# Conformer block on one core: the first chunk's blocks per tile, the last tile in two halves, and one gate multiply moved from GpSimd to VectorE

## The chip, the cores and the metric

The kernel runs on one core of one Trainium2 chip. The metric is the device time of one execution in microseconds (us), as the median of several executions. Each run also leaves a profile of one execution, with the clock that TensorE was granted.

## The reference, cut to what matters

The kernel computes one Conformer block in bf16 on x of shape (2, 4000, 512), with a feed-forward width of 2048 and a depthwise convolution of three taps.

```python
h = _layernorm(x);   x1 = x + 0.5 * (_silu(h @ w_ff1_a) @ w_ff1_b)
h = _layernorm(x1)
attn = softmax((h @ w_q) @ (h @ w_k).T * scale) @ (h @ w_v) @ w_o
x2 = x1 + attn
a, b = split(_layernorm(x2) @ w_pw1)
h = a * _sigmoid(b)                                  # the "gate"
dc = sum(pad(h)[:, i:i + T, :] * dw[i] for i in range(3))   # depthwise, taps dw
dc = (dc - mu) / sqrt(var + 1e-05)                   # mu, var over ALL 8000 rows
x3 = x2 + _silu(dc) @ w_pw2
x4 = x3 + 0.5 * (_silu(_layernorm(x3) @ w_ff2_a) @ w_ff2_b)
return _layernorm(x4)
```

(Abridged; `...` and the batch dimension are left out.) The mean and variance over all rows are what makes a join: nothing behind the convolution can start before the convolution's last chunk has its statistics.

## The kernel before

The 8000 rows are 16 chunks of 500, each of four tiles of 125 rows; the 512 features are four blocks of 128. TensorE is fed from a hand-made order, so the order in the program is the order on each engine.

The start: the first chunk is normalised tile by tile, transposed through TensorE, and its first four blocks of the first product are made as tiles come in.

```python
def head(self):
    self.warm(14)
    self.early = [self.sbank() for _ in range(4)]
    def blocks(lo, hi):                       # tiles lo..hi-1 of the first four blocks
        for f, (ps, b_ps) in enumerate(self.early):
            out = ps[:, lo * TILE:hi * TILE].rearrange("p (t k) -> p t k", t=hi - lo)
            for cc in range(DC):
                self.mm(out, self.Wa[:, cc, f * 128:(f + 1) * 128], self.lnT[0][:, lo:hi, cc, 0:TILE], ...)
    for ti in self.ln_tiles(0, 0, lag=1):
        if ti:
            self.transpose_pe(ti - 1, 0, "ACT", ...)
        if ti == 2:
            blocks(0, 1)
    blocks(1, 2)
    self.transpose_pe(TPC - 1, 0, "DVE", ...)
    blocks(2, 4)
```

The join. `conv_b` and `conv_a` are the two halves of `w_pw1` for one block of features, `gate` is a times sigmoid(b), and `depthwise` is three matmuls with diagonal weights and returns a VectorE statistic and a ScalarE copy. `tail` is the last chunk but one.

```python
def prepare(ti):
    self.project(last, ti)
    if ti == 0:
        self.conv_b(tail, DC - 2)
    if ti == 2:
        self.conv_a(tail, DC - 2)              # gate of block 2, on GpSimd
for ti in self.ln_tiles(last, ..., prepare, ("ACT", "ACT", "DVE", "DVE")):
    if ti == TPC - 3:
        self.conv_b(tail, DC - 1)
        gate = self.conv_a(tail, DC - 1)       # gate of block 3, on VectorE, later
drains = [self.depthwise(tail - 1, self.KEEP)]
for k in range(2):
    self.transpose_pair(k, 1, ("ACT", "DVE")[k], ybank())
drains.append(self.depthwise(tail - 1, DC - 2))
gate()
...
def finish(cc):
    for t in (last, tail):
        f, copy = self.depthwise(t, cc)
        f(); copies.append(copy)
    self.conv_scale(cc)                        # aggregate on VectorE, power on GpSimd
for jj in range(DC):
    self.conv_b(last, jj)
    ...
    self.conv_a(last, jj)
    if jj > 1:
        self.conv_shift(jj - 2)                # needs that power
    if jj:
        finish(jj - 1)
    else: ...                                  # depthwise(tail - 1, DC - 1)
```

The end, `ff_last`: for each tile 16 matmuls of 512 columns, then residual, statistics, factor and normalisation, then the store.

```python
for ti in range(TPC):
    for f in range(FC):
        self.ff_second(f, ti, *blocks[f], f == FC - 1)
    self.residual(...); self.ln_stats(...); self.ln_mean(...); self.ln_factor(...)
    self.ln_norm(c, sl, ti, self.osb[0][:, ti, :], self.b_osb[0][ti], "DVE")
    self.store_out(c, self.osb[0], self.b_osb[0], ti, ti + 1, ("SP", "ACT"))
```

## Time and profile before

| | before |
|---|---|
| time, median of 3 (lowest to highest) | 2060.52 us (2060.18 to 2060.56) |
| span of the profiled execution | 2056.5 us |
| TensorE (PE) busy | 2044.2 us, 99% |
| granted clock over the span | 0.999 |
| VectorE / ScalarE / GpSimd busy | 54% / 36% / 6% |

With TensorE at 99%, the busy shares say nothing on what a small reordering is worth. The list of TensorE's waits does, and the timelines around each wait say who ends it. The prediction shows these lines.

### The profile page before, as it was taken

What the parts mean: (1) busy time and instruction counts of PE and PEld (TensorE: products, weight loads), DVE (VectorE), ACT (ScalarE), POOL (GpSimd) and SP (SyncE); (2) the same over time, 40 slices, a digit from 0 to 9 for tenths busy, and PEclk for the clock granted to TensorE, in tenths of its full rate; (3) what the DMA queues carried; (4) which work ended last, traced back from release to release, by engine and by line L of the source; (5) the groups of instructions that cost most, each with busy time, mean ns of one, the idle gap of its engine ahead of it and who ended that gap; (6) DMA issues with size and microseconds to landing.
All of it is one profiled execution on the core that took longest, in us unless ns stands there. A gap on an engine that the chain in (4) does not pass through costs nothing.

```text
span 2056.5 us, 24392 instructions
## 1 busy us (share of the span) xinstructions
PE 2044.2 (99%) x9653; PEld 1037.7 (50%) x9653; DVE 1110.0 (54%) x2274; ACT 744.3 (36%) x1270; POOL 128.7 (6%) x275
## 2 busy tenths in 40 slices
PE   9999999999999999999999999999999999999998
PEld 5555555554444444444444444444445555555554
DVE  4244444325556667666666676667764443443443
ACT  3433333333333333333333333333345443443432
POOL 2012100000000000000000000000011000000000
PEclk9999999999999999999999999999999999999999
DMA  7232221110001100114301010101143111111111
GB/s 181 54 62 57 56 61 49 46 49 11 16 6 24 24 16 18 21 23 110 92 17 24 18 24 14 23 18 24 38 129 93 31 31 41 31 31 41 31 31 42
DMA packets 209324, 87.73 MB, mean 43 GB/s; under 512 B 157873, under 2 KB 208692, under 8 KB 209204
## 3 DMA queue, kind: packets, MB, share of 16 engines
q1 hardware_dynamic: 208808, 85.79, 17.4%
q8 instruction: 78, 1.28, 0.3%
q14 instruction: 42, 0.34, 0.1%
q10 hardware_dynamic: 396, 0.31, 0.0%
HBM read 29.53 MB, written 19.04 MB: 24 GB/s over the span
## 4 chain that ended last, share of the span: by engine, by line
PE 98%; DVE 1%; issue 0%; POOL 0%; DMA 0%; SPq 0%; ACT 0%; POOLq 0%; DVEq 0%; ACTq 0%
PE s L465 55%; PE y L465 42%; DVE wff L1062 0%; DVE work L547 0%; DMA wff<-in_w_ff_a_dram 0%; DVE xt L680 0%; SPq L519 0%; DVE work L569 0%; POOL work L674 0%; POOL work L1071 0%; DVE wff L967 0%; DVE work L504 0%; ACT work L507 0%; PE y L493 0%; DVE work L1069 0%
## 5 line engine op out<-in xcount | busy, mean ns | idle before, releaser
L507 ACT ACTIVATE work<-s 128x500 bf16<-128x500 f32 (+1 forms) x1060 | 621.6, 587 | 1219.8 <-PE s L465 1218.2
L465 PE MATMUL s<-work,wff 128*128 128x500 bf16 (+2 forms) x2592 | 628.3, 373 | 2.5 <-DVE work L504 1.7
L465 PE MATMUL s<-work,keys 128*128 128x500 bf16 x2048 | 517.5, 374 | 0.1
L465 PE MATMUL y<-work,keys 128*128 128x500 bf16 x2048 | 514.4, 373 | 0.1
L465 PE MATMUL y<-wff,work 128*125 128x512 bf16 x2016 | 506.6, 379 | 0.0
L834 DVE TENSOR_TENSOR work<-work 128x500 f32<-128x500 f32 x496 | 334.4, 674 | 282.1 <-ACT work L507 279.2
L465 PEld LDWEIGHTS s<-work,wff 128*128 128x128 bf16 x2592 | 251.9, 98 | 280.3 <-issue 2.1
L465 PEld LDWEIGHTS y<-wff,work 128*125 128x125 bf16 x2016 | 275.2, 137 | 173.5
L465 PEld LDWEIGHTS y<-work,keys 128*128 128x128 bf16 x2048 | 199.2, 97 | 234.4 <-DVE work L899 1.1
L465 PEld LDWEIGHTS s<-work,keys 128*128 128x128 bf16 x2048 | 199.8, 98 | 232.2 <-DVE work L763 0.6
L680 DVE SCALAR_TENSOR_TENSOR xt<-y,xt 125x512 bf16<-125x512 f32 x128 | 79.7, 683 | 343.8 <-PE y L465 343.8
L547 DVE BATCH_NORM_STATS2 work<-xt 125x6 f32<-125x512 bf16 x316 | 199.7, 680 | 7.9 <-DMA xt<-in_x_dram 7.7
L556 POOL TENSOR_TENSOR work<-work 125x4 f32<-125x4 f32 x76 | 77.0, 1013 | 1115.2 <-DVE work L554 1115.2
L465 PE MATMUL s<-work 128*125 128x512 bf16 (+3 forms) x524 | 133.5, 379 | 2.1 <-DVE work L1172 1.3
L569 DVE TENSOR_SCALAR work<-xt,work 125x512 bf16<-125x512 bf16 x279 | 111.7, 444 | 16.8 <-POOL work L556 13.0
L680 DVE SCALAR_TENSOR_TENSOR xt<-s,xt 125x512 bf16<-125x512 f32 x56 | 38.7, 692 | 146.4 <-PE s L465 146.4
L465 PEld LDWEIGHTS s<-work 128*125 128x125 bf16 (+2 forms) x524 | 70.3, 136 | 47.9 <-issue 3.5
L680 DVE SCALAR_TENSOR_TENSOR xt<-s,work,xt 125x512 bf16<-125x512 f32 x64 | 48.0, 751 | 32.6 <-PE s L465 32.0
L465 PE MATMUL s<-keys,work 128*128 128x500 bf16 x256 | 64.4, 376 | 0.0
L971 DVE SCALAR_TENSOR_TENSOR wff<-wff,s 128x500 bf16<-128x500 f32 x57 | 38.6, 678 | 43.5 <-PE s L465 41.5
L507 ACT ACTIVATE wff<-s 128x500 f32<-128x500 f32 x67 | 39.2, 586 | 57.2 <-PE s L465 55.2
L507 ACT ACTIVATE work<-keys,work 128x500 bf16<-128x500 bf16 x64 | 50.4, 794 | 1.1 <-DVE work L1076 1.1
(89 smaller groups left out, 493.8 us busy)
## 6 DMA issues: line engine op xcount, KB each, us to landing
xt<-in_x_dram SPq DMA_DIRECT2D x15, 500.0 KB
out_dram<-work SPq DMA_DIRECT2D x15, 500.0 KB
dcvd<-wff SPq DMA_DIRECT2D x52, 125.0 KB, 1.7
keys<-dcvd SPq DMA_DIRECT2D x13, 500.0 KB, 4.4
wff<-in_w_ff_a_dram SPq DMA_DIRECT2D x16, 256.0 KB, 4.4
keys<-work SPq DMA_DIRECT2D x8, 512.0 KB, 3.6
keys<-keys SPq DMA_DIRECT2D x32, 128.0 KB, 2.1
work<-work SPq DMA_TRANSPOSE x210, 2.5
```

Source lines behind the costliest of these rows:

```text
L465: self.S.op("PE", lambda e: e.matmul(out, lhsT, rhs, start=start, stop=stop), reads=reads, writes=[bank], inc=stop if inc is None else inc)
L507: return self.S.op("ACT", lambda e: e.activation(out, in_, func, **kw), reads=reads, writes=writes)
L547: self.S.op("DVE", lambda e: e.bn_stats(self.st[sl][:, ti, :], x), reads=[b_x], writes=[self.b_st[sl][ti]])
L556: S.op("POOL", lambda e: e.tensor_tensor(out=self.rs[sl], in0=self.va[sl], in1=self.neghalf[0:TILE, :], op=ALU.pow), reads=self.b_va[sl] + ...
L569: self.S.op("DVE", lambda e: e.tensor_scalar(out, x, self.mv[sl][:, ti, 0:1], self.rs[sl][:, ti:ti + 1], ALU.subtract, ALU.mult), reads=[b ...
L680: self.S.op("DVE", lambda e: e.scalar_tensor_tensor(out=self.XT[g], in0=ps, scalar=scalar, in1=self.XT[g], op0=ALU.mult, op1=ALU.add), rea ...
L834: S.op("DVE", lambda e, p=p: e.tensor_tensor(out=self.acc[s], in0=self.acc[s], in1=self.P[p], op=ALU.add), reads=[self.b_P[p], self.b_acc[ ...
L971: self.S.op("DVE", lambda e: e.scalar_tensor_tensor(out=out, in0=self.th[k], scalar=1.0, in1=ps[:, 0:CHUNK], op0=ALU.add, op1=ALU.mult), r ...
```

## The change

Its intent is to shorten three places in which TensorE waits. At the start each tile's 16 small matmuls run as soon as that tile is there. At the join one gate multiply moves from GpSimd to VectorE, three depthwise matmuls leave the wait in front of the last chunk and each shift moves behind the next statistic. At the end the last tile's second product is made in two halves of 256 columns, so that half of the residual and of the statistics runs beside the other half's matmuls.

```diff
-        def blocks(lo, hi):
+        def blocks(ti):
...
-                    self.mm(out, ..., self.lnT[0][:, lo:hi, cc, 0:TILE], ...
+                    self.mm(ps[:, ti * TILE:(ti + 1) * TILE], ..., self.lnT[0][:, ti, cc, 0:TILE], ...
...
-            if ti == 2:
-                blocks(0, 1)
-        blocks(1, 2)
+            if ti > 1:
+                blocks(ti - 2)
         self.transpose_pe(TPC - 1, 0, "DVE", (self.Yb[TPC - 1], self.b_Y[TPC - 1]))
-        blocks(2, 4)
+        blocks(TPC - 2)
+        blocks(TPC - 1)
... (ff_last: the last tile)
+        for n in range(2):
+            d = slice(n * D // 2, (n + 1) * D // 2)
+            ps, b_ps = self.Yb[(0, ti)[n]], self.b_Y[(0, ti)[n]]
+            ... 16 matmuls into ps[0:TILE, d], residual and bn_stats of those columns
+            if n == 0:
+                out(TPC - 2)
+        ... one aggregate over both statistics, factor, out(ti)
... (join)
-            if jj < DC - 1:
+            if jj < DC - 2:
                 return gate("POOL")
             return lambda: gate("DVE")
...
-            if ti == 2:
-                self.conv_a(tail, DC - 2)
+            if ti == 1:
+                gates.append(self.conv_a(tail, DC - 2))
...
-        drains.append(self.depthwise(tail - 1, DC - 2))
-        gate()
+        for gate in gates:
+            gate()
...  (in finish)
+                if t == last and cc > 1:
+                    self.conv_shift(cc - 1)
...
-                f, copy = self.depthwise(tail - 1, DC - 1)
-                f()
-                copies.append(copy)
+                for cc in (DC - 2, DC - 1):
+                    f, copy = self.depthwise(tail - 1, cc)
+                    f()
+                    copies.append(copy)
```

## The prediction

> **What bounds the kernel now.** I read the engines' busy time first, then TensorE's waits, then the timelines around those waits. Columns of the timelines: start, us, engine, line, operation, output<-inputs, count, [idle before <- releaser].

> ```profile
> PE 2044.2 (99%) x9653; PEld 1037.7 (50%) x9653; DVE 1110.0 (54%) x2274; ACT 744.3 (36%) x1270; POOL 128.7 (6%) x275
> ```

> ```profile
> PE s L465 <- DVE work L504: 1.7, 3, 0.9
> PE s L465 <- DVE work L1172: 1.3, 1, 1.3
> PE s L465 <- ACT work L507: 1.0, 2, 0.8
> PE y L493 <- ACT work L507: 1.0, 1, 1.0
> PE s L465 <- DMA wff<-in_w_ff_a_dram: 0.6, 1, 0.6
> ```

> TensorE is busy 2044.2 of 2056.5 us, and the span's granted clock is 0.999. The waits listed (total, times, longest) and two of 0.4 and 0.3 us sum to 6.3 us; with 5.3 us after TensorE's last matmul (2051.17 to 2056.5), where only VectorE, GpSimd and a store still run, that is all that any reordering can win: under 0.6%. All these waits lie in three places: the first 13 us, the join between attention and the second feed-forward (1535 to 1564 us), and the last 6 us. The change touches exactly these. Everything between runs TensorE back to back, so what is won in one place should reach the end.

> Start, the blocks of the first chunk:

> ```profile
> 10.74 0.39 PE L480 MATMUL y<-work 125*128 125x125 bf16 x4
> 11.16 0.42 DVE L504 COPY work<-y 128x500 bf16<-128x500 bf16 x1 [2.21 <-PE y L480]
> 11.73 2.73 PE L465 MATMUL s<-work,wff 128*128 128x250 bf16 x20 [0.61 <-DVE work L504]
> 12.36 2.73 ACT L507 ACTIVATE work<-s 128x500 bf16<-128x500 f32 x5 [1.71 <-PE s L465]
> ```

> The blocks of tiles 2 and 3 (16 matmuls of 250 columns) wait together for the copy of tile 3, though tile 2 was ready at 10.64.

> The join:

> ```profile
> 1533.06 1.25 POOL L957 TENSOR_TENSOR wff<-wff 128x500 bf16<-128x500 f32 x1 [0.21 <-ACT wff L507]
> 1533.57 0.75 DVE L620 SCALAR_TENSOR_TENSOR work<-work 125x1 f32<-125x1 f32 x1
> ...
> 1551.54 0.25 DVE L1069 BATCH_NORM_AGGREGATE work<-wff 128x2 f32<-128x21 f32 x1
> ...
> 1551.87 0.55 POOL L1071 TENSOR_TENSOR work<-work 128x1 f32<-128x1 f32 x1 [1.49 <-DVE work L1069]
> ...
> 1552.52 0.16 DVE L1076 SCALAR_TENSOR_TENSOR work<-work 128x1 f32<-128x1 f32 x1 [0.73 <-POOL work L1071]
> ...
> 1556.06 1.08 PE L465 MATMUL s<-work 128*125 128x512 bf16 x4 [0.84 <-ACT work L507]
> ```

> Two stalls of VectorE: an instruction on one column takes 0.75 us and ends (1534.32) just after GpSimd's gate multiply (1534.31); and VectorE idles 0.73 us between the aggregate of block 2 and its shift, because the shift needs a GpSimd power. The chain of waits runs along VectorE from there to the swish that releases TensorE at 1556.06.

> End: the last tile's residual, statistics and so on are serial after TensorE's last matmul.

> ```profile
> 2049.24 1.89 PE L465 MATMUL y<-wff,work 128*125 128x512 bf16 x8
> ...
> 2051.17 0.69 DVE L680 SCALAR_TENSOR_TENSOR xt<-y,xt 125x512 bf16<-125x512 f32 x1 [0.55 <-PE y L465]
> 2051.89 0.69 DVE L547 BATCH_NORM_STATS2 work<-xt 125x6 f32<-125x512 bf16 x1
> 2052.62 0.18 DVE L667 BATCH_NORM_AGGREGATE work<-work 125x2 f32<-125x6 f32 x1
> ```

> [...] The trace's start-to-start times agree: 54.5, 107.3, and 215.5 for 512. [...] weight loads of 125 columns show 137 ns against 98 for 128. Even so both overlap the matmuls, so halving the columns should not bring the load on the path: eight matmuls of one column with 125-column weights stand 58.3 ns apart, under 109. [...] The 746 ns above against 148 to 160 for its six siblings agrees. [...] The trace agrees in slope: 683 ns for 512 columns, 150 for one.

> **The start.** With tile 2 alone, its 16 matmuls follow the transposes of tile 3 at about 10.96 and take 16 x 0.0545 = 0.87, to 11.83. Tile 3's copy ends at 11.58 and releases TensorE some 0.15 later (as before: 11.58 to 11.73), so the 16 of tile 3 run from 11.83 to 12.70 without waiting. Before, block 4 began at 11.73 + 16 x 0.1073 = 13.44. But block 4 needs the PSUM bank of block 0, which ScalarE frees: its first block is complete at 11.83 + 3 x 0.0545 + 0.22 = 12.21, the activation (0.59, 0.04 after) ends at 12.84, TensorE goes on at 12.98. Gain 0.74 - 0.28 = **0.46 us**. The next weights landed at 10.77 and later chunks land over 2 us before use, so no transfer takes it back.

> **The join.** (a) The gate of block 2 leaves GpSimd: 1245 ns less there, 671 on VectorE (as the gate of block 3 took), but placed behind the pair copy, where VectorE would soon wait. (b) conv_a of block 2 goes ahead of the projection of tile 2, which ends 0.86 later (1532.37 against 1531.51); VectorE reaches its residual at 1532.41 instead of 1532.13: a loss of 0.28. (c) The one-column instruction shrinks from 0.75 to 0.15: a win of 0.60. Sum to the last normalise and so to the pair copy: 0.32 earlier; the first matmuls of the last chunk start at 1538.36 instead of 1538.68. (d) Before, three depthwise matmuls (0.63 us) filled the wait in front of that copy. Now they follow the chunk's first eight matmuls, so the second eight start at 1538.36 + 1.70 + 1.27 = 1541.34 against 1541.03, and with them VectorE's second gate, which waits for exactly this: 1543.30 against 1542.99. The 0.32 are gone, and 0.31 lost. ScalarE gets to the first sigmoid one copy earlier, but that isn't the last wait here. (e) From there the chain gate, two statistics, aggregate, GpSimd power, halo, gate repeats as before, 0.31 late, to the last gate (1549.75 against 1549.44). (f) The shifts move behind the next statistics. Shift 1 waited for nothing and, between two statistics, hides a gap: the aggregate of block 2 starts 1551.77 against 1551.54. Shift 2's wait of 0.73 is now filled with a statistic of 0.68: statistic 1551.95 to 1552.63, shift at 1552.76, next statistic 1552.83 instead of 1553.31. So 0.48 won at the end of the chain, and the aggregate, power, shift and swish behind it keep that: swish at 1554.73 instead of 1555.21. ScalarE, with its copies and swishes, is free at 1554.3 by the same count, TensorE before that. The four swishes and normalisations that follow are back to back on ScalarE, hence shift along. Net **0.48 us**.

> **The end.** 32 matmuls x 0.1095 = 3.50 instead of 16 x 0.216 = 3.46: lose 0.05. The first half is complete about 1.75 us before the second; its residual and statistics (0.42 each) and the normalise of tile 2 (0.41) fit in, done at about 2050.8, before the second half at 2051.2. After the last matmul the residual and the statistics fall by 256 columns each[...]: win 0.53. The aggregate over two groups costs some 0.03 more (15 values took 0.222 us, 6 took 0.176). Net **0.45 us**.

> Sum: 0.46 + 0.48 + 0.45 = 1.39 us of 2060.52, so 2059.1.

> **Rivals.** (1) The join gives nothing or costs: (d) is a real loss on TensorE, and if the statistic that fills the wait of shift 2 has to wait for its own matmuls (they need ScalarE copies that stand behind an activation table load of 1.28 us), the win shrinks. For: before, TensorE waited at 1550.65 for just such a copy. Against: I place that copy's end at 1550.90 and the matmuls' at 1551.76, before the aggregate's end at 1552.02, but the slack is only 0.2 us. Time then 2059.6. (2) ScalarE keeps the start as it was: if the activation rather than the matmuls paced blocks 4 and on. Against: it starts one every 0.47 us there, TensorE asks every 1.7. For: half of the gain is already lost to it in my sum. Time 2059.3 to 2059.5. (3) The end gains more, if the store of tile 2, now nearer to the last one, doesn't matter, and less if weight loads show at 256 columns (32 x 28 ns, the gap between 137 and 109, would be 0.9 us, eating the whole half): 2060.0. The pitch of 58 ns speaks against it. (4) The join gains up to 0.9, if the second gate isn't as late as in (d), since ScalarE alone would allow the swish at 1554.3: 2058.7.

> **Range and chances.** Run to run is 0.4 us. Each part may be off by 0.2 to 0.4, mostly independently, so 0.7 each way: 2058.4 to 2059.9. All the waits together are under 0.6% and the added matmuls 16, so leaving the 2% band is all but excluded: 0.003 each way.

> **What would show it.** Right: no wait of TensorE on the VectorE copy near 11.8 but about 0.3 on ScalarE before block 4; no one-column instruction of 0.7 us; all gates from the second on about 0.3 later relative to the start of the join, and the swish of the last block 0.5 earlier; the last residual and statistics near 0.42 each. Wrong: a wait for weights at the start, TensorE's matmuls of 256 columns over 0.115 apart, or the last depthwise statistic waiting for TensorE.

54.5, 107.3 and 215.5 ns are the start-to-start times of matmuls of 125, 250 and 512 columns. The 109 ns for 256 columns (0.1095 us in the sum of the end) are my estimate, near the line from 107.3 to 215.5; the changed kernel's trace then had 109.2. That the instruction of 746 ns would shrink to 0.15 us is my estimate too, from its six siblings of 148 to 160 ns and from its end beside that of GpSimd's multiply; why it takes longer there was not shown. The 0.53 us of the end follow from 683 ns for 512 columns and 150 for one: 1.04 ns a column, so 0.267 us for 256 columns, twice.

## More of the kernel before

The taps of the convolution are loaded in the second chunk, and TensorE turns them round six steps later; the change doesn't touch this, the argument does:

```python
if c == 1 and f == 1:
    self.load(self.dwr, i["dw"], [self.b_dwr])
    self.after(6, self.taps)
```

Last, the whole program is followed by a conditional second program for data out of range, which doesn't run here. Each engine therefore ends by loading a flag and taking a branch:

```python
self.program(False)
fits = nc.values_load(self.flag, ...)
self.wait_out()
with nc.If(fits < 1):
    self.program(True)
```

## The result, and the profile after

The changed kernel took 2060.77 us (median of 4 runs: 2061.31, 2060.21, 2060.23, 2063.35), the kernel before 2060.54 us (2060.18 to 2060.61, 4 runs). A ratio in this document is the mean time of one kernel's runs over that of the other's of the same rounds, so it isn't quite the ratio of the medians: here 1.0004, with a 95% interval of 0.9987 to 1.0021. The predicted 2059.1 us and the range of 2058.4 to 2059.9 were wrong. None of the four runs lies in the range. Two of them, 1.1 and 3.1 us above the other two, differ by more than the kernel before's runs here.

First the page of the changed kernel, engines' busy time:

```profile
PE 2045.9 (99%) x9685; PEld 1039.7 (51%) x9685; DVE 1112.8 (54%) x2277; ACT 744.4 (36%) x1270; POOL 127.0 (6%) x274
```

The 32 more matmuls and the GpSimd instruction less are the change. But TensorE is busy for 1.7 us longer (2044.2 before), although 16 matmuls of 512 columns became 32 of 256. TensorE's waits in the changed kernel (total, times, longest):

```profile
PE s L465 <- DVE work L504: 1.7, 2, 0.9
PE s L465 <- DVE work L1196: 1.3, 1, 1.3
PE y L480 <- ACT work L507: 0.7, 1, 0.7
PE s L465 <- DMA wff<-in_w_ff_a_dram: 0.6, 1, 0.6
PE y L493 <- ACT work L507: 0.6, 1, 0.6
```

The wait on the tile copy near 11.8 us is gone (the first line had three waits, now two), and with it the wait of 0.8 us on a ScalarE swish at 1556 us. The total of the first line stays at 1.7 us because its other wait, in front of the last chunk of the join, grew from 0.23 to 0.87 us: step (d) of the prediction leaves it unfilled. So the waits went as foreseen and the time didn't. The timeline of the start, changed kernel (start, us, engine, line, operation, output<-inputs, count, [idle before <- releaser]):

```profile
11.15 3.04 PE L465 MATMUL s<-work,wff 128*128 128x125 bf16 x36
11.35 0.42 DVE L504 COPY work<-y 128x500 bf16<-128x500 bf16 x1 [2.23 <-PE y L480]
...
14.03 0.59 PE L465 MATMUL y<-wff,work 128*125 128x512 bf16 x2
```

The 16 matmuls of tile 2 run beside tile 3's copy, and those of tile 3 follow without a gap. From tile 3's transposes (10.93) to the first matmul of the second product (14.03) it is 3.10 us; before it was 3.56 (10.74 to 14.29, in rounded times).

At the join, the timeline of the changed kernel:

```profile
1533.58 0.15 DVE L620 SCALAR_TENSOR_TENSOR work<-work 125x1 f32<-125x1 f32 x1
...
1538.08 3.29 PE L465 MATMUL s<-work,wff 128*128 128x500 bf16 x8 [0.87 <-DVE work L504]
```

The one-column instruction takes 0.15 us instead of 0.75, and the first eight matmuls of the last chunk start earlier. But these eight take 3.29 us. The same eight before:

```profile
1538.68 1.86 PE L465 MATMUL s<-work,wff 128*128 128x500 bf16 x8 [0.23 <-DVE work L504]
```

The windows from 1538 to 1542 us say why. Columns: us, then PE, PEld, DVE, ACT and POOL busy with the count of instructions, the granted TensorE clock, DMA share, GB/s. Kernel before:

```profile
1538.00:1542.00 4.00, 3.77 (x19) 1.51 (x17) 2.87 (x5) 2.17 (x4) 0.45 (x4) 1.00 0.37 120
```

Changed kernel:

```profile
1538.00:1542.00 4.00, 3.92 (x11) 1.52 (x12) 2.23 (x4) 1.06 (x2) 1.07 (x6) 0.57 0.29 92
```

TensorE was as busy and did 11 matmuls instead of 19, because its clock was 0.57 of full speed on average. In the records of the clock it was 0.5 from 1538.33 us for 3.41 us, then full again.

The end, changed kernel:

```profile
2052.22 0.42 DVE L757 SCALAR_TENSOR_TENSOR xt<-y,xt 125x256 bf16<-125x256 f32 x1 [0.61 <-PE y L465]
2052.68 0.43 DVE L760 BATCH_NORM_STATS2 work<-xt 125x6 f32<-125x256 bf16 x1
2053.14 0.21 DVE L763 BATCH_NORM_AGGREGATE work<-work 125x2 f32<-125x12 f32 x1
```

Residual and statistics fell from 0.69 to 0.42 and 0.43 us as predicted. Yet the span ends 2.88 us after the last normalisation, which ends at 2054.62; before it was 2.42 us. The transfers in the two microseconds from that point (queue, kind, packets, MB, share of the 16 engines), kernel before and then changed kernel:

```profile
q1 hardware_dynamic: 96, 0.08, 17.0%
q10 hardware_dynamic: 60, 0.05, 6.9%
q14 instruction: 2, 0.02, 2.3%
```

```profile
q1 hardware_dynamic: 93, 0.08, 17.4%
q10 hardware_dynamic: 59, 0.05, 7.3%
q8 instruction: 1, 0.02, 3.8%
```

q1 and q10 carry the last store. Beside it the changed kernel has one packet of q8, an instruction fetch, that the kernel before does not have there, and of its 156 store packets only 152 fall in the window.

To see where time goes, I cut each trace at four marks: the first one-column matmuls of the last softmax sums, at the end of attention ("start", near 1525 us; called "the sums" below), the first of the second feed-forward ("join", near 1564), the end of the last normalisation ("last tile") and the end of the span ("store"). Each entry is the length of that stretch less its length in the kernel before, to about 0.01 us; the runs other than "after" are the experiments below.

| trace | start | join | last tile | store | sum |
|---|---|---|---|---|---|
| predicted | -0.46 | -0.48 | -0.45 | 0 | -1.39 |
| after | -0.27 | +1.22 | -0.40 | +0.47 | +1.02 |
| again | +0.74 | -0.47 | -0.39 | +0.21 | +0.09 |
| filled | +0.20 | -0.46 | -0.40 | +0.92 | +0.26 |
| head_tail | +0.34 | 0.00 | -0.40 | +0.81 | +0.75 |
| drain_moved | -0.59 | +0.60 | +0.01 | +0.08 | +0.10 |
| taps_later | -0.53 | -0.46 | -0.39 | +0.59 | -0.79 |
| tail_128_384 | -0.76 | -0.47 | -0.10 | +0.02 | -1.31 |
| tail_pad | -1.00 | -0.48 | -0.39 | -0.16 | -2.03 |
| fixed_pad | -0.97 | -0.45 | -0.40 | +0.08 | -1.74 |
| before_taps | -0.13 | +0.01 | +0.01 | +0.02 | -0.09 |
| join_alone | +0.21 | -0.46 | 0.00 | +0.08 | -0.17 |
| wait_1 | -0.88 | +0.27 | -0.39 | +0.50 | -0.50 |
| wait_1_again | -0.98 | +0.24 | -0.39 | +0.26 | -0.87 |
| wait_2 | -0.53 | +2.65 | -0.39 | +0.75 | +2.48 |
| wait_3 | -0.40 | +4.63 | -0.39 | +0.78 | +4.62 |
| wait_3_filled | -0.31 | +1.70 | -0.39 | +0.43 | +1.43 |

The start has a scatter of its own, since the first loads land at different times (TensorE waits 0.6 us for the first weights in the kernel before, 0.2 in before_taps, and drain_moved lists no such wait): drain_moved and before_taps have the old start and lie 0.5 us apart. So the start is better read from inside: tile 3's transposes to the first block of the second product took 3.56 us in all four traces with the old start and 3.10 in all thirteen with the new one. The predicted 0.46 us is there every time. From that block to the mark near 1525 us it is 1510.63 or 1510.64 us in fifteen of the seventeen traces, and 1511.96 and 1511.79 in again and head_tail, so the gain reaches the end of attention except in these two.

### The profile page after: what moved, and what is told of

It is laid out like the page before. It is cut to its first block, busy times and chain, and to the rows that moved or that the text cites. A ratio compares the mean times of both kernels' runs of the same rounds, so it can differ in the third digit from the quotient of the medians.

```text
span 2057.5 us, 24459 instructions
## 1 busy us (share of the span) xinstructions
PE 2045.9 (99%) x9685; PEld 1039.7 (51%) x9685; DVE 1112.8 (54%) x2277; ACT 744.4 (36%) x1270; POOL 127.0 (6%) x274
## 3 DMA queue, kind: packets, MB, share of 16 engines
q8 instruction: 78, 1.28, 0.3%
## 4 chain that ended last, share of the span: by engine, by line
PE 98%; DVE 1%; issue 0%; POOL 0%; DMA 0%; SPq 0%; ACT 0%; POOLq 0%; DVEq 0%; ACTq 0%
PE s L465 55%; PE y L465 42%; DMA wff<-in_w_ff_a_dram 0%; DVE work L547 0%; DVE wff L1086 0%; SPq L519 0%; DVE work L569 0%; POOL work L674 0%; POOL work L1095 0%; DVE xt L680 0%; DVE wff L991 0%; ACT work L507 0%; DVE work L504 0%; PE y L493 0%; DVE work L1093 0%
## 5 line engine op out<-in xcount | busy, mean ns | idle before, releaser
L507 ACT ACTIVATE work<-s 128x500 bf16<-128x500 f32 (+1 forms) x1060 | 621.8, 587 | 1219.1 <-PE s L465 1217.6
L465 PE MATMUL s<-work,wff 128*128 128x500 bf16 (+1 forms) x2608 | 629.9, 373 | 2.7 <-DVE work L504 1.7
L465 PE MATMUL s<-work,keys 128*128 128x500 bf16 x2048 | 517.5, 374 | 0.1
L465 PE MATMUL y<-work,keys 128*128 128x500 bf16 x2048 | 514.4, 373 | 0.1
L465 PE MATMUL y<-wff,work 128*125 128x512 bf16 (+1 forms) x2024 | 506.8, 378 | 0.0
L465 PEld LDWEIGHTS s<-work,wff 128*128 128x128 bf16 x2608 | 252.4, 98 | 280.8 <-issue 2.9
L465 PEld LDWEIGHTS y<-wff,work 128*125 128x125 bf16 x2024 | 275.9, 136 | 172.8
L465 PEld LDWEIGHTS y<-work,keys 128*128 128x128 bf16 x2048 | 199.2, 97 | 234.4 <-DVE work L923 1.1
L465 PEld LDWEIGHTS s<-work,keys 128*128 128x128 bf16 x2048 | 199.8, 98 | 232.2 <-DVE work L787 0.6
L680 DVE SCALAR_TENSOR_TENSOR xt<-y,xt 125x512 bf16<-125x512 f32 x127 | 79.1, 683 | 340.4 <-PE y L465 340.4
L547 DVE BATCH_NORM_STATS2 work<-xt 125x6 f32<-125x512 bf16 x315 | 199.1, 680 | 8.1 <-DMA xt<-in_x_dram 7.9
L465 PE MATMUL s<-work 128*125 128x512 bf16 (+3 forms) x524 | 133.3, 379 | 1.3 <-DVE work L1196 1.3
L680 DVE SCALAR_TENSOR_TENSOR xt<-s,xt 125x512 bf16<-125x512 f32 x56 | 38.7, 692 | 146.3 <-PE s L465 146.3
L465 PEld LDWEIGHTS s<-work 128*125 128x125 bf16 (+2 forms) x524 | 70.2, 136 | 47.0 <-issue 3.3
L680 DVE SCALAR_TENSOR_TENSOR xt<-s,work,xt 125x512 bf16<-125x512 f32 x64 | 48.1, 751 | 32.6 <-PE s L465 32.0
L465 PE MATMUL s<-keys,work 128*128 128x500 bf16 x256 | 64.4, 376 | 0.0
L507 ACT ACTIVATE wff<-s 128x500 f32<-128x500 f32 x67 | 39.2, 587 | 58.3 <-PE s L465 56.2
L507 ACT ACTIVATE work<-keys,work 128x500 bf16<-128x500 bf16 x64 | 50.4, 795 | 0.4 <-DVE work L1100 0.4
```

The costliest lines, as they stand in the source:

```text
L465: self.S.op("PE", lambda e: e.matmul(out, lhsT, rhs, start=start, stop=stop), reads=reads, writes=[bank], inc=stop if inc is None else inc)
L507: return self.S.op("ACT", lambda e: e.activation(out, in_, func, **kw), reads=reads, writes=writes)
L547: self.S.op("DVE", lambda e: e.bn_stats(self.st[sl][:, ti, :], x), reads=[b_x], writes=[self.b_st[sl][ti]])
L680: self.S.op("DVE", lambda e: e.scalar_tensor_tensor(out=self.XT[g], in0=ps, scalar=scalar, in1=self.XT[g], op0=ALU.mult, op1=ALU.add), rea ...
```

## The experiments

My theory after the result: each part gains what it should, and three leaks take it back: a late load behind the start, the half clock in the join, and the instruction fetch beside the last store. The main rivals: a part gains nothing by itself (the parts disturb each other), and what I saw is the chance of one profiled execution.

The first four ran together; the kernel before took 2060.50 us beside them (median of 9 runs, 2060.34 to 2061.88).

**again**: the changed kernel, no edit.

> The changed kernel, unaltered, to see how it varies. Theory (clock): TensorE's clock is halved for one stretch of 3.41 us in the join, in the executions where its measuring window happens to hold the emptied wait; such runs take 2061.0 or more, the others 2060.3 or less, and the trace shows a granted clock near 0.57 at 1538 to 1542 us only if its own time is of the first kind. Rival (no gain to be had in the join): the time does not depend on the granted clock there, and the runs scatter without two levels.

Measured: 2060.84 us (five runs, 2060.35 to 2062.92), ratio 1.0003 (0.9989 to 1.0017). The join is at full clock and gains 0.47 us, so the half clock is not in every execution. The two groups of times that I expected did not come: one run is at 2060.35 us, three between 2060.68 and 2060.92 and one at 2062.92. And there is a new wait at 46.8 us, by the waits and the timeline of this run:

```profile
PE s L465 <- DMA work<-in_dw_dram: 1.3, 1, 1.3
```

```profile
46.83 0.25 PE L465 MATMUL s<-work 3*128 3x3 bf16 x4 [1.26 <-DMA work<-in_dw_dram]
```

These are the taps of the convolution, a load of 3 KB issued at 39.48 us that landed at 46.79. In the kernel before it was issued at 38.24 and landed at 45.68, and the same four matmuls started with no wait:

```profile
46.09 0.25 PE L465 MATMUL s<-work 3*128 3x3 bf16 x4
```

In this run TensorE was 0.6 us earlier at the first block of the second product (13.71 against 14.29 us), and the load was issued 1.2 us later: it stands in the queue of SyncE behind other transfers (three transposed loads, whose issue ended at 38.35 us here and at 37.12 in the kernel before), and its time does not follow TensorE's. In the kernel before 0.4 us lay between the landing and the use (46.09 - 45.68). Arriving earlier wins nothing there, and when the load is late, the start's gain and more is lost.

**filled**: the changed kernel with seven useless matmuls in TensorE's idle time in the join.

```diff
+    def fill(self, n):     # n matmuls of resident weights into the next bank, which is overwritten anyway
+        for k in range(n):
+            self.mm(self.Sb[r][:, 0:CHUNK], self.Wp1[:, 0, 0:128], self.Wp1[:, 0, 0:CHUNK], ...)
...
-            self.transpose_pair(k, 1, ("ACT", "DVE")[k], ybank())
+            self.transpose_pair(k, 1, ("ACT", "DVE")[k], ybank(), (3, 0)[k])   # 3 between tiles 0 and 1
+        self.fill(4)
```

> The changed kernel with seven matmuls of no use (3 + 4 of 500 columns) in the two waits of TensorE just before the last chunk's blocks. Theory (clock): no stretch at half clock in the join, the second eight matmuls of the last chunk at full rate, runs within 0.5 us of each other, median 2059.2 to 2060.0. Rival (the moved depthwise matmuls and GpSimd's halos cost what the shifts win, whatever the clock): as the changed kernel, 2060.2 to 2061.3.

Measured: 2061.63 us (2060.72 to 2064.91), ratio 1.0008 (0.9994 to 1.0021). The trace keeps the full clock and gains the 0.46 us in the join. The median lies above my range and above the rival's: the time did not improve, and one run of 2064.91 us shows that there are slow executions that the half clock cannot explain. As a remedy of the time this failed; the store stretch is the longest of all (+0.92).

**head_tail**: the kernel before with the start and the end of the change, without the join. The edit is the first two parts of the diff above:

```diff
-        blocks(2, 4)
+        blocks(TPC - 2)
+        blocks(TPC - 1)
... (all of head and of ff_last; nothing of the gates, the depthwise matmuls and the shifts)
```

> Only the start and the end of the change, the join as before. Theory (the end's gain of 0.5 us goes to a later last store, because TensorE's branch and its fetches of instructions come later against the end): last packets of the last store land 0.4 to 0.9 us later after the last normalise than before, median 2060.0 to 2060.3. Rival (the end is sound, only the join failed): 2059.5 to 2059.8. The join shows no half clock in either.

Measured: 2061.34 us (2060.40 to 2062.06), ratio 1.0002 (0.9988 to 1.0016). The start's gain is again lost to the taps, and the last tile gains 0.40 us while the store loses 0.81, within the 0.4 to 0.9 that I expected. The median is above both ranges; the expectation had left out the taps.

```profile
46.44 0.25 PE L465 MATMUL s<-work 3*128 3x3 bf16 x4 [1.09 <-DMA work<-in_dw_dram]
```

So the start and the end, with the old join, are worth nothing as they stand.

**drain_moved**: the kernel before, with only the three depthwise matmuls of block 2 moved out of the wait, as the change does.

```diff
-        drains.append(self.depthwise(tail - 1, DC - 2))
...
-                f, copy = self.depthwise(tail - 1, DC - 1)
-                f()
-                copies.append(copy)
+                for cc in (DC - 2, DC - 1):
+                    f, copy = self.depthwise(tail - 1, cc)
+                    f()
+                    copies.append(copy)
```

> The kernel before with one step alone: the three depthwise matmuls of block 2 leave the wait before the last chunk's blocks and follow them. Theory (clock): some executions show a half clock of 3.41 us at the join and take 2062.0 to 2062.6; the others lose 0.3 us, 2060.8. Rival (the moved matmuls matter only as work): 2060.8 in all, clock 1.00 throughout the join.

Measured: 2060.96 us (2060.62 to 2063.73), ratio 1.0005 (0.9991 to 1.0018). The join is 0.60 us longer at full clock, and TensorE's wait in front of the last chunk grew from 0.23 to 0.87 us:

```profile
1538.08 1.86 PE L465 MATMUL s<-work,wff 128*128 128x500 bf16 x8 [0.87 <-DVE work L504]
```

This is step (d) of the prediction by itself: a real loss of 0.6 us, close to the 0.63 counted there and twice the 0.3 of the expectation. The half clock that I expected in some executions is not in this trace, and the run of 2063.73 us left no trace.

The next four try to close the leaks. They ran together, beside them the kernel before took 2060.58 us (9 runs, 2059.68 to 2061.82).

**taps_later**: the changed kernel, with TensorE asking for the taps 14 us later.

```diff
-                    self.after(6, self.taps)
+                    self.after(12, self.taps)
```

> The changed kernel with the tap transposes six blocks later (from about 46 us to about 56). Theory (the start's gain is eaten at 46 us, where TensorE needs a 3 KB load that lands when the transposing queue lets it): no wait for that load, the first-chunk gain of 0.3 to 0.6 us still there when attention starts; runs without a half clock take 2059.9 to 2060.6, a little less than the changed kernel's. Rival (the start's gain is lost elsewhere before attention): attention starts no earlier than with the wait, about 455.0.

Measured: 2060.29 us (2058.95 to 2061.80), ratio 0.9998 (0.9984 to 1.0012). There is no wait on the taps, and from the first block of the second product to the end of attention it is 1510.64 us, so the start's gain stays. (The -0.53 of the table alone wouldn't show it: drain_moved has -0.59 with the old start.) The store still takes 0.59 us.

**tail_128_384**: taps_later, with the last tile cut into 128 and 384 columns.

```diff
-            d = slice(n * D // 2, (n + 1) * D // 2)
+            d = slice(0, 128) if n == 0 else slice(128, D)
```

> As the run with later taps, and the last tile in pieces of 128 and 384 columns instead of 256 and 256. Theory (fetch): TensorE reaches its branch some 0.9 us earlier against the end, its second instruction fetch begins about 0.7 us before the last normalise ends, and the last store's packets end 1.6 to 1.75 us after it, as before the change; 0.27 us of the halves' gain is given up. Rival (the last store is later because the store before it is nearer, or because of the split itself): packets still end 1.9 to 2.5 after the normalise.

Measured: 2059.37 us (2058.84 to 2059.78), ratio 0.9993 (0.9979 to 1.0006). The last tile gains only 0.10 us, since 384 columns follow the last matmul, but the store is as before (+0.02). The second fetch on q8 starts 0.93 us ahead of the last normalisation's end.

**tail_pad**: taps_later with the two equal halves, and 17 useless matmuls behind the last real one.

```diff
         self.ln_factor(sl, ti)
         out(ti)
+        for k in range(17):
+            self.mm(self.Sb[r][:, 0:CHUNK], self.Wb[:, 0, 0:128], self.Wb[:, 0, 0:CHUNK], ...)
```

> As the run with later taps, and 17 matmuls of no use after the last real one, so that TensorE comes to its branch later. Theory (fetch): the second instruction fetch begins 2 us or more after the last normalise, the store's packets end about 1.6 after it, the end of the span follows the normalise by 2.4 to 2.5 us instead of 2.6 to 3.3; 0.3 to 0.8 us less than with later taps alone. Rival (the split or the nearer stores): packets end 1.9 to 2.5 after the normalise, time as with later taps.

Measured: 2058.90 us (2058.86 to 2059.97), ratio 0.9993 (0.9979 to 1.0006). Its trace has the matmuls beside the last normalisation:

```profile
2049.53 3.75 PE L465 MATMUL s<-wff 128*128 128x500 bf16 x17
...
2049.80 0.42 DVE L757 SCALAR_TENSOR_TENSOR xt<-y,xt 125x256 bf16<-125x256 f32 x1 [0.62 <-PE y L465]
```

The last tile keeps its 0.39 us and the store is 0.16 us shorter than before, 0.75 shorter than in taps_later. The median is 1.39 us under that of taps_later, more than the 0.3 to 0.8 that I expected; the rest is not explained. What the useless matmuls do can be read from the records of TensorE's sequencer. In the kernel before it reaches the branch at the program's end 6.41 us before the last normalisation ends. With halves of 256 columns it is 4.06 us, since the 17 matmuls and 16 weight loads that still start after it has begun to load the flag are shorter ones. With the 17 matmuls it is 2.18. From the branch on, two fetches of 16 KB follow on q8, the first some 1.0 to 1.4 us and the second 4.1 to 4.8 us after the branch starts. The branch, with the first of them in it, took 3.4 to 3.9 us in the seventeen traces; those of VectorE, GpSimd, ScalarE and SyncE took 45 to 72 ns in the kernel before. The second fetch hits the last store or misses it:

| trace | second fetch, from the last normalisation's end | store packets end |
|---|---|---|
| before, before_taps, join_alone, drain_moved | -1.74 to -1.87 | +1.58 to +1.63 |
| tail_128_384 | -0.93 | +1.59 |
| after, again, filled, head_tail, taps_later and five runs below | +0.17 to +0.77 | +1.90 to +2.54 |
| tail_pad, fixed_pad | +2.15 to +2.20 | +1.59, +1.60 |

A fetch lasts 0.95 to 1.46 us, and the store's packets start from +0.89 us on. Where the fetch lies in that stretch, 8 to 12 of the 156 store packets end after +1.64 us, elsewhere none. How the fetch delays them was not shown, since the packed trace doesn't number the DMA engines. The profile counts 16 of them, and 156 / 16 is some ten packets, so my estimate is that one engine's packets wait. In all seventeen traces the store is late exactly where the fetch lies just before it.

**fixed_pad**: taps_later with the matmuls of both filled and tail_pad.

> Later taps, seven filling matmuls in the join's waits, and the 17 after the last: the three leaks closed together. Theory: 2059.0 to 2059.7, spread under 0.6 us except where the first loads of the kernel land late; start -0.46, join -0.48, end -0.4 against the kernel before can be read from the trace. Rival (something else takes the gain): 2060.2 or more.

Measured: 2059.58 us (2058.81 to 2060.00), ratio 0.9994 (0.9980 to 1.0008). The median is in the expected range, the spread of 1.2 us is double the expected one, and the filling of the join brings nothing on top.

The next four take the controls and ask for the cause of the half clock. The kernel before took 2060.98 us beside them (9 runs, 2060.20 to 2062.66).

**before_taps**: the kernel before with the edit of taps_later alone.

> The kernel before with one edit, the preparation of the taps six steps later. My theory: the kernel before has about 0.3 us of slack at the load of the taps, so the edit gives it nothing in most executions: 2060.5 us, ratio 0.9998 to 1.0002, the marks from the attention on within 0.3 us of the kernel before once the first loads' jitter is taken off. Rival: the load costs the kernel before something too (its slower executions of 2061 to 2062 us), so that the taps are an improvement of their own: median 2060.0 us or less, and none of five over 2061 us.

Measured: 2060.35 us (2059.84 to 2060.61), ratio 0.9996 (0.9982 to 1.0010). The trace differs by 0.09 us from the kernel before, as I expected. But no run of five is over 2061 us, while four of nine of the kernel before are. The rival had that right: the load seems to cost the kernel before too in some executions. With no trace of one of those, this stays an indication.

**join_alone**: the kernel before with the join's edits alone, which are the last part of the diff above, from the gate's condition on:

```diff
-            if jj < DC - 1:
+            if jj < DC - 2:
                 return gate("POOL")
... (and all that follows it; nothing of head and of ff_last)
```

> The kernel before with the join's edits only. My theory: between the first matmuls of the sums and the first block of the second feed-forward 0.47 us are won wherever TensorE keeps its full clock, start and end stay as before, and the store ends 2.4 us after the last normalise as before: median 2060.0 us, with single executions up to 1.7 us longer where the granted clock falls by half. Rival (the join is worth nothing by itself): 2060.5 us, and the stretch is as long as before.

Measured: 2060.07 us (2059.61 to 2061.55), ratio 0.9995 (0.9982 to 1.0009). The join gains 0.46 us by itself, start and end are as before. The filled wait of the shift, in this trace:

```profile
1552.13 0.62 DVE L1062 BATCH_NORM_STATS2 wff<-y 128x6 f32<-128x500 f32 x1
...
1552.95 0.16 DVE L1076 SCALAR_TENSOR_TENSOR work<-work 128x1 f32<-128x1 f32 x1 [0.19 <-POOL work L1071]
```

The shift's idle time fell from 0.73 to 0.19 us, because a statistic now runs in it.

**wait_1** and **wait_3**: taps_later, with the VectorE copy that TensorE waits for in front of the last chunk made twice and four times, so that TensorE idles longer.

```diff
-        self.away(eng, dst, src, b_ps, self.b_lnT[s][2 * k:2 * k + 2])
+        for _ in range(2 if (k, s) == (1, 1) else 1):      # wait_3: 4
+            self.away(eng, dst, src, b_ps, self.b_lnT[s][2 * k:2 * k + 2])
```

> The changed kernel with later taps, and the VectorE copy that releases the first matmuls of the last chunk made twice, so that TensorE waits 0.68 us longer there. If the half clock is set off by how little TensorE does in the stretch before these matmuls (my theory), it should come more often than without: the trace shows about 0.5 granted clock for 3.4 us in the join with some probability, and the times split into a group near 2061.0 (2060.3 + 0.7) and one near 2062.7. Rival (the half clock has nothing to do with this wait, or is a chance of that execution): one group near 2061.0 us.

Measured for wait_1: 2060.47 us (2060.18 to 2061.01), ratio 0.9997 (0.9983 to 1.0011); the trace is at full clock. The rival's single group fits, my two groups do not.

> As the last, with the copy made four times, so that TensorE waits 2.05 us longer, some 2.9 us in all. My theory: TensorE is then almost idle for over 4 us and the half clock comes in nearly every execution: the matmuls of 500 columns behind it stand 415 ns apart for up to 3.4 us, the stretch from the sums to the second feed-forward is 1.6 + 1.7 = 3.3 us longer than before, and the median is 2060.3 + 2.05 + 1.7 = 2064.0 us. Rival (clock not tied to the wait): matmuls 212 ns apart, the stretch 1.6 us longer than before, and 2062.3 us.

Measured for wait_3: 2063.61 us (2063.05 to 2065.26), ratio 1.0010 (0.9997 to 1.0024). Every run is above the rival's 2062.3 us. The profiled run, the slowest, had 0.5 clock from 1539.30 for 6.83 us, two windows instead of one, so the join is 4.63 us longer and not the 3.3 expected. The eight matmuls in it:

```profile
1540.11 3.49 PE L465 MATMUL s<-work,wff 128*128 128x500 bf16 x8 [3.03 <-DVE work L505]
```

By this the cause was likely but not shown, since the wait came along with the emptiness. Three more ran, with the kernel before at 2060.88 us beside them (9 runs, 2060.14 to 2061.47).

**wait_3_filled**: wait_3 with 3 and 13 useless matmuls in the idle time, by the code of filled.

> The kernel with three more copies in the wait, and useless matmuls put into TensorE's idle time: three between the transposes of the first two tiles, thirteen behind those of the last. The chain of VectorE copies is as long as there. My theory (TensorE's emptiness halves the clock): the clock stays at 1.00, the eight matmuls behind the wait take 1.86 us as in the kernel before, and the median is 2060.3 + 2.05 = 2062.3 us with none of five over 2063.5 us. Rival (the long wait itself or the work behind it does it): half clock again, 2063.6 us as without the filling.

Measured: 2061.84 us (2061.18 to 2064.13), ratio 1.0008 (0.9994 to 1.0022).

```profile
1537.02 2.91 PE L465 MATMUL s<-wff 128*128 128x500 bf16 x13
1540.21 1.86 PE L465 MATMUL s<-work,wff 128*128 128x500 bf16 x8 [0.29 <-DVE work L514]
```

The chain of copies is as long as in wait_3, the clock stays full (1.00 from 1534 to 1546 us, where wait_3 falls to 0.50), and the join is 1.70 us longer than before instead of 4.63. So in these two traces it is TensorE's emptiness that halves the clock, not the wait. One run of 2064.13 us breaks my bound: a slow execution of another kind, as in filled.

**wait_2**: two more copies.

> Two more copies in the wait (1.37 us). Theory of the grid: the clock is set anew every 3.413 us from how busy TensorE was in the window just ended, with the limit between 0.54 (fell) and 0.60 (did not) of the window by the fourteen traces. Then over three quarters of the executions should show half a clock, and the trace shows it exactly where a window of the grid, counted back from the fall of the clock after the kernel's end, was less busy than 0.54: 2061.7 us without, 2062.3 to 2063.4 us with. Rival (limit is far lower, or not busy time at all): the trace at full clock although such a window was under 0.54, and a median of 2061.7 us or less.

Measured: 2062.34 us (2061.02 to 2063.21), ratio 1.0005 (0.9991 to 1.0019). Three of five runs are at 2062.3 or more, fewer than the over three quarters that the theory of the grid wanted. The trace has its least busy window (0.30) from 1535.93 to 1539.35 and half a clock for the 3.41 us behind it:

```profile
1539.26 3.44 PE L465 MATMUL s<-work,wff 128*128 128x500 bf16 x8 [2.31 <-DVE work L505]
```

**wait_1_again**: wait_1 without an edit.

> The kernel with one more copy, unchanged, for a second trace with another place of the grid. Theory of the grid: its least busy possible window is 0.33, and about three quarters of the places have one under 0.54, so the trace is probably at half clock in the join, and several of five runs lie over 2061.5 us. Rival: five runs near 2060.5 us again, and full clock.

Measured: 2061.03 us (2059.59 to 2062.02), ratio 1.0003 (0.9989 to 1.0016). Full clock, so the likelier outcome did not come. But the least busy window of its grid at this wait was 0.64 (0.65 in wait_1; a later one, at 1560.7 us, was 0.62), for in both executions the idle time was shared out on two windows. So the rule holds for the two traces, and my odds do not: a slid grid has a window under 0.545 in 0.76 of its places here, and the five runs of wait_1, up to 2061.01 us, leave hardly any room for the 1.7 us of a half clock.

## Why the prediction was wrong

**What bounds the kernel.** The reading of the waits was right, and they went as foreseen. The step that failed is "Everything between runs TensorE back to back, so what is won in one place should reach the end". TensorE ran back to back past the taps at 46 us only because it came 0.4 us after their load. A wait that isn't in the list of waits can still be that near. With the taps later, the start's gain reached the end of attention in all nine traces. The same step took the clock for granted in the join and the time behind the last normalisation for unchanged.

**The start.** The mechanism and the size were right: 0.46 us predicted and 0.46 measured, in every trace. Block 4, held up by ScalarE, starts 0.327 us after the matmul in front of it instead of 0.0545, so 0.27 us late (0.28 predicted; the wait of 0.2 us on ScalarE in the list of waits is another one, at 8 us). What failed is "so no transfer takes it back": I had looked at the weights of the next chunks and not at the 3 KB of taps, which cost 1.26 and 1.09 us in two traces.

**The join.** Steps (a) to (f) were right at full clock. In again the first eight matmuls come 0.33 us earlier, measured from the sums (0.32 predicted), the second eight 0.28 later (0.31), and the stretch is 0.47 us shorter (0.48). Rival (1), a statistic that waits for its matmuls, did not happen, nor did rival (4), a smaller loss in (d). What failed is in (d): the three depthwise matmuls were counted as 0.63 us that change place, but in the wait they also kept TensorE busy enough for its clock (least busy window 0.63 with them at full clock, 0.54 in the changed kernel's profile, followed by half a clock). Where the grid fell badly, as in the profiled execution, the join was 1.22 us longer instead of 0.47 shorter, so the half clock cost 1.69 us. That two runs of four and one of five of the changed kernel were slow fits with this, but only one of them has a trace, and the kernel before, whose windows don't get below 0.61, has runs of up to 2062.66 us too. Sliding the grid over the trace puts a window of under 0.545 in about a quarter of its places. At 1.69 us each that is an estimate of 0.4 us on average, nearly what the join wins. The estimate may be too high: of the ten runs of tail_128_384 and tail_pad, with the same join, none is over 2060 us.

**The end.** The last tile gained 0.39 to 0.40 us with the equal halves (0.45 predicted). The pitch of the 256-column matmuls did not grow (109.2 ns in the changed kernel's trace, beside weight loads of 136), and the aggregate cost 0.21 instead of 0.18 us, as counted. What failed is that the sum stops at the last normalisation, as if the store behind it took as long as before; rival (3) thought of the store of tile 2 alone. The halves shorten the last 33 instructions of TensorE, so its sequencer reaches the branch 2.35 us later relative to the store (6.41 - 4.06), and the branch's fetch falls on the store: 0.2 to 0.9 us lost in the ten traces, 0.57 on average, where 0.39 was won.

**The sum.** The three parts won 0.46, 0.47 and 0.39 us, together 1.32. An estimate of what they ran into, from the figures above: 0.57 us at the store, 0.6 at the taps (1.32 and 1.15 in two of the four traces with the new start and the old taps), and some 0.4 for the clock. That is 1.2 us without the clock and 1.6 with it, so nothing is left, as measured. With the leaks at the taps and the store closed, tail_pad took 2058.90 us, 1.7 us less than the kernel before beside it, and 0.2 from the predicted 2059.1. Its trace holds the three parts and 0.16 us at the store, 1.48 in all. So the 1.39 us were there to be had; the prediction missed what they would run into. But that the time came out so near is in part luck, since the later taps alone gave the kernel before a median 0.6 us lower. tail_pad beats both kernels by its median, though the interval of its ratio includes 1.

**What stays open.** Between 0.54 and 0.60 the limit of the clock is bracketed, by the least busy windows of seventeen traces, three of them with half a clock; a busy share counted with other weights would fit as well. In wait_3 a second half window followed one that was 0.76 busy at half speed. With the transposes left out, the same traces put the limit between 0.18 and 0.24, and a slid grid then falls under it in 0.39 to 0.51 of the places for wait_1 and 0.60 to 0.72 for wait_2, nearer to their runs than 0.76 and 0.97. So which work counts, and how often the changed kernel is hit, is not settled. Runs of up to 2064.91 us in filled and 2064.13 in wait_3_filled, whose traces have no window under 0.61, remain unexplained, since a run that was not profiled leaves no trace. I did not run the later taps and the 17 matmuls with the old join.

## What to carry to other kernels

A gain on a saturated engine is only as long as the shortest slack behind it (here 0.4 us at the taps): before counting it at the end, look for loads that land just before they are used, and move their use. Work that fills a wait on TensorE may also be holding its clock up, so take it out only where the rest stays busy: here a window of 3.41 us that was 0.54 busy was followed by half a clock, which cost 1.69 us, and none of 0.60 or more at full clock was. And the last microseconds belong to every engine, also to the instruction fetch of one that has long finished: here it cost the store 0.57 us on average of ten traces.
